# A fused attention, gating-MLP and expert kernel on one core: earlier W_out loads, earlier third-batch input, copies of Q in another order

## The chip, the core and the metric

The kernel runs on one core of a Trainium2 chip. The metric is device time in microseconds, the median of the runs shown. The core has a matrix engine (PE, with its weight loads shown as PEld), three engines for elementwise work (DVE, ACT, POOL) and a queue for transfers on SyncE (SP); ACT issues some transfers too. All of them run at the same time and meet through semaphores.

## What is computed

Three layers in a row, all in float32, with 4 batches of 576 tokens and 512 features:

```python
def reference(q, k, v, ...):
    # stage 1: attention with rotated q and k, 8 heads of 64
    q_rot, k_rot = rotate(q), rotate(k)
    scores = q_rot @ k_rot.T / sqrt(64)
    x = softmax(scores) @ v                      # heads side by side: 4 x 576 x 512
    # stage 2: MLP with a gate over the tokens
    h = gelu(x @ w_in)                           # 512 -> 1024
    u, v = h[..., :512], h[..., 512:]
    v_n = (v - mean(v)) / sqrt(var(v) + 1e-6) * g_ln
    v_s = einsum('ts,bsd->btd', w_sg, v_n) + b_sg
    x = x + (u * v_s) @ w_out
    # stage 3: four experts, each a causal attention with one head of 64; two of four per token
    for e in range(4):
        q, k, v = x @ wq[e], x @ wk[e], x @ wv[e]
        ye = softmax(causal(q @ k.T / 8)) @ v @ wo[e]
        out += weight_of_expert(x @ w_gate, e) * ye
```

## The kernel before

Every product is done in three matmuls: each float32 operand is split into a high part and a low part (`split`: ACT casts the high part, POOL, sometimes DVE, subtracts it for the low part), and `mm3` adds high x high, high x low and low x high. So every tile that PE takes as an operand needs a cast on ACT and a subtraction on POOL or DVE ahead of it. In tile names the letter h is the high part, l the low part: xh and xl are the split input of stage 2, gxh and gxl the split gated product, wuh and wul the split W_out, yh and yl the split input of stage 3, hi and lo those of a projection of Q or K.

PE, ACT, DVE and POOL keep the order in which the program is written while the flag `fixed` is set (class `Engine`), so an instruction that waits holds back all that stand behind it on its engine. Transfers on SP are placed by the scheduler, and SP issues them in that order; a transfer that waits for its source or its buffer holds back those behind it.

Stage 2 is written as units, each a generator that first issues PE's matmuls and then, step by step, the work on the other engines; `unit` advances the two units before it and takes side steps in between. For each batch b there are `values(b, tb)` (five blocks of tokens, matmuls into ps_t and ps_S), `gates_(b, dc)` (four feature chunks, results in the tiles u), `added(b - 1, dc)` (W_out's product of the batch before, plus the input, which is loaded as xr<-xd; the sum is stored to yd) and `mixed(b, dc)` (the product over the tokens, with the weights wsh and wsl and the operands vh and vl, and the gate: DVE scales by gl, adds bs and multiplies by u). Beside the units run side generators:

- `attended(bx, b + 1)`, the next batch's input in twelve steps: load (sa<-xr, sl<-xr, and sr, which is three transfers), norm (a multiplication on POOL, and a store to xd) and part (the split into xh and xl) for each of four chunks. The tiles sa have three buffers. For b = 1 this is the third batch. In the loop over b, the number of steps that a unit takes of it stands in a tuple.
- `leftover`, the last 64 tokens of two batches at once (ea, er, eh, el).
- `lu`, the loading and splitting of W_out by chunks of rows: a transfer on ACT's queue (raw), a conversion by ACT into the scratch bank ps_c, integer steps on DVE in ps_c, then wt, wuh and wul.
- `normalized(b)`, which makes vh and vl from the values.

gl and bs are the gate's scale and offset, loaded by SP and halved by DVE once.

Stage 3 goes through the pairs n = 0 to 7 (two experts of one batch each). `qkproj` makes the projections of Q and K of the next pair; Q's high and low parts are taken to the operands q2 and qz by six transfers on SP (`fill_q`), four of which read hi. The tile hi has one buffer, so the cast of K into hi waits until these four have read it. `parts_of(b)` loads and splits the stage's input (x, then yh and yl) in steps; the table `INPUT_AT` says in which slots of a pair they are taken, its first row for n = 0.

Of the kernel before, what the change touches and what calls it, by code (L numbers as in the profile page):

```python
# [12 lines left out]
ALU = mybir.AluOpType  # L13
AX = mybir.AxisListType

B, H, S, D = 4, 8, 576, 64
# [10 lines left out]
def f(ap):  # L27

    return ap.bitcast(F32)
# [4 lines left out]
QK_AT = (0, 1, 3, 3, 4, 4)  # L34
FINISH_AT = ((7, 8), (4, 5))
VALUES_AT = (1, 4)
INPUT_AT = ((0, 1, 2, 3, 5, 6), (1, 3, 5, 7), (2, 4))


@with_exitstack  # L40
def fused_kernel(ctx, tc, qk, v, w_in, w_out, w_sg, g_ln, b_sg, wqk, wvg, wo, rope, cst, out):
# [17 lines left out]
    PE, ACT, DVE, POOL = Engine(nc.tensor), Engine(nc.scalar), Engine(nc.vector), Engine(nc.gpsimd)  # L59
# [9 lines left out]
    def bank(t):  # L69
        shape = [P, 2, 512] if t.isupper() else [P, 512]  # L70
        return ps[t].tile(shape, F32, tag="b", name="ps_" + t)
# [12 lines left out]
    def halves(t):  # L84
        return [(t[:, c, 0:HS], slice(HS * c, HS * c + HS)) for c in range(2)]
# [12 lines left out]
    def mm3(o, chunks):  # L98


        n = len(chunks)
        for ci, (lh, ll, rh, rl) in enumerate(chunks):
            for pi, (l, r) in enumerate(((lh, rh), (lh, rl), (ll, rh))):
                for (t, sl) in o:
                    PE.matmul(t, l, r[:, sl], start=(ci == 0 and pi == 0),
                              stop=(ci == n - 1 and pi == 2))
            yield


    class Pair:  # L110
# [41 lines left out]
        def fill_q(self, qh, ql):  # L152
            q2, qz = self.q2, self.qz
            a, c = slice(0, 64), slice(64, 128)
            todo = [(q2[a, 0, 0:S], qh[a, :]), (q2[c, 0, 0:S], ql[a, :]), (qz[a, 0], qh[a, :])]
            if self.turned:
                todo += [(q2[c, 1, 64:640], qh[c, :]), (q2[a, 1, 64:640], ql[c, :]), (qz[c, 1], qh[c, :])]
            else:
                todo += [(q2[c, 1, 0:512], qh[c, 0:512]), (q2[a, 1, 0:512], ql[c, 0:512]),
                         (qz[c, 1, 64:S], qh[c, 0:512])]  # L160
                for o, i in ((q2[c, 1, 576:640], qh[c, 512:576]), (q2[a, 1, 576:640], ql[c, 512:576]),
                             (qz[c, 1, 0:64], qh[c, 512:576])):
                    POOL.tensor_copy(o, f(i))
            for (o, i) in todo:
                nc.sync.dma_start(f(o), f(i))
# [93 lines left out]
    def run(gen):  # L259
        for _ in gen:  # L260
            pass
# [83 lines left out]
    with ExitStack() as st:  # L345
# [30 lines left out]
        class Work:  # L376
# [53 lines left out]
            def values(self):  # L430
                self.vst = ld2.tile([P, NKB, 2, P], F32R, tag="vst", name="vst")
                ACT.copy(self.vst[:, :, :, 0:D], self.vt)
                POOL.tensor_tensor(self.vst[:, :, :, D:P], self.vt, f(self.vst[:, :, :, 0:D]), op=ALU.subtract)
# [266 lines left out]
    with ExitStack() as st:  # L700
# [8 lines left out]
        gl = wp.tile([P, 4], F32, name="gl")  # L709
        bs = wp.tile([P, S], F32, name="bs")  # L710
# [137 lines left out]
        def added(b, dc):  # L848

            gh, gll = gs[b]  # L850
            sl = slice(P * dc, P * dc + P)
            t = bank("S")
            xr = wk.tile([P, S], F32, tag="u", name="xr", bufs=5) if dc % 2 else ge.tile([P, S], F32, tag="ga", name="xr", bufs=2)
            nc.sync.dma_start(xr, xd[b][dc])
            run(mm3(halves(t), [(wu[0][:, c, sl], wu[1][:, c, sl], gh[:, c], gll[:, c]) for c in range(4)]))
            yield
            DVE.tensor_tensor(hv(xr), t[:, :, 0:HS], hv(xr), op=ALU.add)
            nc.sync.dma_start(yd[b][dc], xr)
# [4 lines left out]
        def unit(g, *side, then=iter(()), n=0):  # L863


            next(g)
            todo = [s for s, k in side for _ in range(k)]
            a, b = [[t] for t in taken]
            while a or b:
                if a:  # L870
                    x = next(a[0], LATER)
                    if x is LATER:
                        a = []
                if b:
                    if next(b[0], LATER) is LATER:
                        b = []
                if todo:
                    next(todo.pop(0), None)
            for s in todo + n * [then]:
                next(s, None)  # L880
            taken[:] = [g, taken[0]]
# [4 lines left out]
        lu = load_split64(wst, *wu, w_out, 0, nc.scalar.dma_start, POOL, 2, lambda: bank("c"))  # L886
# [3 lines left out]
        at = nsteps  # L890
        for tb in range(2, NKB):
            unit(values(0, tb), (lw, 2), (at, (1, 1, 1)[tb - 2]))
            if tb == 2:
                DVE.tensor_scalar(gl, gl, 0.5, None, op0=ALU.mult)
                DVE.tensor_scalar(bs, bs, 0.5, None, op0=ALU.mult)
        ln = normalized(0)
        unit(gates_(0, 0), (lw, 2), (at, 2))
        unit(gates_(0, 1), (lw, 2), (at, 2))
# [3 lines left out]
        unit(gates_(0, 3), (ln, 2))  # L902
        run(at)
        run(lw)

        for tb in range(2):
            unit(values(1, tb), then=ln, n=1)
# [3 lines left out]
        for b in range(1, B):  # L911
            at = attended(bx, b + 1) if b + 1 < B else iter(())
            for tb in range(0 if b > 1 else 2, NKB - b % 2):
                unit(values(b, tb), (lu, 3), (at, (1, 2, 2, 1, 0)[tb]))
            ln = normalized(b)
            for dc in range(4):
                unit(gates_(b, dc), (lu, 2), (ln, (0, 0, 1, 1)[dc]), then=ln, n=(0, 2, 0, 0)[dc])
            run(lu)
            if b == 2:
                w = wc.tile([P, 12, DM], F32R, tag="w", name="w")  # L920
                wq, wo_ = [w[:, 0:4], w[:, 4:8]], [w[:, 8:10], w[:, 10:12]]
                side = itertools.chain(load_split(wst, *wq, wqk), load_split(wst, *wo_, wo))
            elif b == B - 1:
                wbs.close()
                cr = ExitStack()
                one, ld, cy = [cr.enter_context(tc.tile_pool(name=n, bufs=k, side="right", reuse_waits="tile"))
                               for n, k in (("c_one", 1), ("c_ld", 2), ("c_y", 1))]
                prs3 = [Pair(one, x, ident) for x in range(2)]
                ypools.append(cy)
                xtile[0] = lambda: wst.tile([P, 1024], F32, tag="raw", name="x", bufs=2)[:, 0:640]  # L930
                wg = wtile(one, "wg", 4, 260)
                side = itertools.chain(parts_of(0), load_split(wst, *wg, wvg))
            else:
                side = leftover(bx, b + 1)
            for dc in range(4):
                unit(added(b - 1, dc), (ln, (1, 2, 1, 2)[dc]), (at, (0, 1, 1, 2)[dc]))
            for dc in range(4):
                unit(mixed(b, dc), (at, 1), (side, 5))
            run(at)
            run(side)  # L940
# [8 lines left out]
    with ExitStack() as st:  # L949
# [319 lines left out]
        def slot3(k):  # L1269
# [100 lines left out]
            if (n + 1) // 2 + 1 < B:  # L1370
                if k == 0 or pp and x == 0:
                    ys.append(parts_of((n + 1) // 2 + 1))
                if x in INPUT_AT[min(n, 2 - pp)]:
                    next(ys[-1], None)
# [114 lines left out]
```

## Time and profile before

| | us |
|---|---|
| runs | 713.23, 714.21, 714.75 |
| median | 714.21 |
| profiled execution | 711.89 |
| its span | 710.1 |
| PE busy in the span | 679.1 (96%) |
| DVE, ACT, POOL busy | 493.9, 462.1, 382.3 |

Stage 1 runs to about 285 us of the span, stage 2 from there to about 517 us, and stage 3 to the end. Times below are in microseconds from the start of the span, and all of one profiled execution. A timeline row gives the start, the duration of one merged group of equal instructions, the engine, the line (L55 is the helper that issues everything on the compute engines), the operation with its output and inputs, and the count. Where the engine was idle just ahead of it, the square bracket has the idle time and what ended it. A row of stretches has the busy time of each engine in it, and the clock that was granted to PE as a share of full speed (PEclk).

### The profile page before, as it was taken

Reading aid. Unit: us, or ns where it says so; the run is one execution under the profiler, and the core shown is the slowest. Engines: PE = TensorE matmul, PEld = TensorE weight load, DVE = VectorE, ACT = ScalarE, POOL = GpSimd, SP = SyncE. Lnnn points to the kernel's source line nnn. Section 1 sums busy time; section 2 is a strip of 40 time slices with the busy share of each in tenths; the row PEclk is TensorE's granted clock in tenths of the full one; section 3 lists DMA queues with packets and bytes.
Section 4 is the critical chain, followed back from the end, with each engine's and each line's share of the span. In section 5 each row is a group of like instructions: output and inputs, shape, how many; then the busy total and the mean of one; then the engine's idle time right before and its main releaser. Section 6 shows DMA issues by size and latency. Waiting matters only on the chain.

```text
span 710.1 us, 13966 instructions
## 1 busy us (share of the span) xinstructions
PE 679.1 (96%) x4813; PEld 608.0 (86%) x4813; DVE 493.9 (70%) x1063; ACT 462.1 (65%) x1110; POOL 382.3 (54%) x353
## 2 busy tenths in 40 slices
PE   7799999999999999999999999999998989999996
PEld 6688887878788888798898799899998979999875
DVE  5797879898979888487873574565247666656674
ACT  7687878878788888574472362572146666666673
POOL 1889788888899873661536507306222443342320
PEclk9899999999999999999999999999999999999999
DMA  8568898878887865562365424045455354442521
GB/s 305 158 160 233 252 292 255 231 230 247 245 240 237 230 179 144 167 176 66 107 199 175 137 79 135 29 134 153 114 169 133 88 149 114 116 124 63 137 83 66
DMA packets 69896, 116.31 MB, mean 164 GB/s; under 512 B 21025, under 2 KB 30082, under 8 KB 69826
## 3 DMA queue, kind: packets, MB, share of 16 engines
q1 hardware_dynamic: 67090, 109.75, 53.9%
q10 hardware_dynamic: 2736, 5.68, 2.6%
q8 instruction: 38, 0.62, 0.4%
q14 instruction: 32, 0.26, 0.1%
HBM read 60.05 MB, written 21.08 MB: 114 GB/s over the span
## 4 chain that ended last, share of the span: by engine, by line
PE 40%; DVE 5%; DMA 2%; ACT 1%; POOL 1%; issue 1%; SPq 1%; ACTq 0%; DVEq 0%
PE ps_S L55 25%; PE ps_o L55 5%; PE ps_f L55 4%; PE ps_t L55 4%; PE ps_s L55 3%; DMA xr<-xd 1%; DVE ps_c L55 1%; DMA yd<-xr 1%; DVE e L55 1%; POOL gxl L55 1%; POOL sa L55 0%; DVE h1l L55 0%; ACT e L55 0%; DVE u L55 0%; DVE xt L55 0%
## 5 line engine op out<-in xcount | busy, mean ns | idle before, releaser
L55 DVE TENSOR_REDUCE nmax<-ps_S 128x1 f32<-128x576 f32 x144 | 107.8, 748 | 26.7 <-PE ps_S L55 26.3
L55 PE MATMUL ps_t<-ident,e 128*128 128x128 f32 x776 | 121.9, 275 | 4.3 <-ACT e L55 2.8
L55 ACT ACTIVATE e<-ps_S,nmax 128x576 f32<-128x576 f32 x144 | 107.5, 746 | 28.3 <-DVE nmax L55 27.1
L55 PEld LDWEIGHTS ps_t<-ident,e 128*128 128x128 f32 x776 | 95.3, 141 | 9.8 <-ACT e L55 4.5
L55 POOL TENSOR_TENSOR t<-t,rp 128x576 f32<-128x576 f32 x61 | 93.0, 1546 | 14.4 <-ACT rp L55 9.2
L55 PE MATMUL ps_S<-kh,q 128*128 128x288 f32 x352 | 81.7, 325 | 11.3 <-ACT e L55 4.2
L55 PEld LDWEIGHTS ps_S<-kh,q 128*128 128x128 f32 x352 | 53.5, 191 | 35.2 <-ACT e L55 18.5
L55 PE MATMUL ps_S<-lo,qz 128*128 128x288 f32 x304 | 66.4, 300 | 1.5 <-DVE lo L55 1.5
L55 POOL TENSOR_TENSOR lo<-t,hi 128x576 fp32r<-128x576 f32 x30 | 42.8, 1428 | 29.2 <-DVE hi L55 15.3
L55 PE MATMUL ps_S<-yh,w 128*128 128x288 f32 x256 | 51.5, 304 | 1.3 <-DVE nmax L55 1.3
L55 ACT ACTIVATE e<-e,nmax 128x128 f32<-128x128 f32 (+4 forms) x72 | 42.2, 586 | 14.0 <-DVE nmax L55 13.8
L55 PEld LDWEIGHTS ps_S<-lo,qz 128*128 128x128 f32 x304 | 49.7, 192 | 1.7 <-DVE lo L55 1.7
L55 POOL TENSOR_TENSOR yl<-x,yh 128x640 fp32r<-128x640 f32 x16 | 25.5, 1594 | 42.7 <-ACT yh L55 40.8
L55 POOL TENSOR_TENSOR t<-t 128x576 f32<-128x576 f32 x29 | 42.5, 1464 | 2.3
L55 PE MATMUL ps_o<-g,v 128*64 128x320 f32 x256 | 41.3, 445 | 0.0
L55 PEld LDWEIGHTS ps_S<-yh,w 128*128 128x128 f32 x256 | 38.7, 189 | 1.5 <-DVE nmax L55 1.5
L55 ACT ACTIVATE ga<-ga 128x512 f32<-128x512 f32 (+1 forms) x34 | 22.3, 656 | 24.0 <-DVE ga L55 23.7
L55 PE MATMUL ps_S<-wsh,vh 128*128 128x288 f32 x160 | 34.6, 298 | 1.7 <-DVE u L55 1.4
L55 POOL TENSOR_TENSOR xl<-sa,xh 128x576 fp32r<-128x576 f32 x12 | 18.2, 1522 | 30.7 <-ACT xh L55 30.7
L55 PE MATMUL ps_S<-wsl,vh 128*128 128x288 f32 x160 | 34.1, 294 | 0.0
L55 POOL TENSOR_TENSOR gxl<-u,gxh 128x576 fp32r<-128x576 f32 x16 | 22.8, 1433 | 19.5 <-ACT gxh L55 19.5
L55 DVE CUSTOM_DVE_ANT_0 e<-ps_s,mask 128x128 f32<-128x128 f32 (+3 forms) x64 | 30.9, 482 | 3.2 <-PE ps_s L55 2.9
(302 smaller groups left out, 2020.6 us busy)
## 6 DMA issues: line engine op xcount, KB each, us to landing
t<-in_qk_dram SPq DMA_DIRECT2D x32, 576.0 KB
kh<-hi SPq DMA_DIRECT2D x92, 144.0 KB
q<-hi SPq DMA_DIRECT2D x38, 144.0 KB
qz<-hi SPq DMA_DIRECT2D x38, 144.0 KB
q<-lo SPq DMA_DIRECT2D x38, 144.0 KB
v<-in_v_dram SPq DMA_DIRECT2D x16, 320.0 KB
sa<-xr SPq DMA_DIRECT2D x16, 288.0 KB
xd<-sa SPq DMA_DIRECT2D x16, 288.0 KB
```

Source lines behind the costliest of these rows:

```text
L55: ins = op(*a, **k)
```

## The change

Four edits: the first row of `INPUT_AT`; the order of the six transfers in `fill_q`; the place of the halving of gl and bs, together with one more step of `lu` ahead of it; and the tuples that give the third batch's input its steps.

```diff
@@ -34,7 +34,7 @@
 QK_AT = (0, 1, 3, 3, 4, 4)
 FINISH_AT = ((7, 8), (4, 5))
 VALUES_AT = (1, 4)
-INPUT_AT = ((0, 1, 2, 3, 5, 6), (1, 3, 5, 7), (2, 4))
+INPUT_AT = ((0, 1, 2, 3, 4, 6), (1, 3, 5, 7), (2, 4))
 
 
 @with_exitstack
@@ -152,12 +152,13 @@
         def fill_q(self, qh, ql):
             q2, qz = self.q2, self.qz
             a, c = slice(0, 64), slice(64, 128)
-            todo = [(q2[a, 0, 0:S], qh[a, :]), (q2[c, 0, 0:S], ql[a, :]), (qz[a, 0], qh[a, :])]
+            todo = [(q2[a, 0, 0:S], qh[a, :]), (qz[a, 0], qh[a, :])]
             if self.turned:
-                todo += [(q2[c, 1, 64:640], qh[c, :]), (q2[a, 1, 64:640], ql[c, :]), (qz[c, 1], qh[c, :])]
+                todo += [(q2[c, 1, 64:640], qh[c, :]), (qz[c, 1], qh[c, :]), (q2[a, 1, 64:640], ql[c, :])]
             else:
-                todo += [(q2[c, 1, 0:512], qh[c, 0:512]), (q2[a, 1, 0:512], ql[c, 0:512]),
-                         (qz[c, 1, 64:S], qh[c, 0:512])]
+                todo += [(q2[c, 1, 0:512], qh[c, 0:512]), (qz[c, 1, 64:S], qh[c, 0:512]), (q2[a, 1, 0:512], ql[c, 0:512])]
+            todo.append((q2[c, 0, 0:S], ql[a, :]))
+            if not self.turned:
                 for o, i in ((q2[c, 1, 576:640], qh[c, 512:576]), (q2[a, 1, 576:640], ql[c, 512:576]),
                              (qz[c, 1, 0:64], qh[c, 512:576])):
                     POOL.tensor_copy(o, f(i))
@@ -890,9 +891,6 @@
         at = nsteps
         for tb in range(2, NKB):
             unit(values(0, tb), (lw, 2), (at, (1, 1, 1)[tb - 2]))
-            if tb == 2:
-                DVE.tensor_scalar(gl, gl, 0.5, None, op0=ALU.mult)
-                DVE.tensor_scalar(bs, bs, 0.5, None, op0=ALU.mult)
         ln = normalized(0)
         unit(gates_(0, 0), (lw, 2), (at, 2))
         unit(gates_(0, 1), (lw, 2), (at, 2))
@@ -902,6 +900,9 @@
         unit(gates_(0, 3), (ln, 2))
         run(at)
         run(lw)
+        next(lu)
+        DVE.tensor_scalar(gl, gl, 0.5, None, op0=ALU.mult)
+        DVE.tensor_scalar(bs, bs, 0.5, None, op0=ALU.mult)
 
         for tb in range(2):
             unit(values(1, tb), then=ln, n=1)
@@ -911,7 +912,7 @@
         for b in range(1, B):
             at = attended(bx, b + 1) if b + 1 < B else iter(())
             for tb in range(0 if b > 1 else 2, NKB - b % 2):
-                unit(values(b, tb), (lu, 3), (at, (1, 2, 2, 1, 0)[tb]))
+                unit(values(b, tb), (lu, 3), (at, (1, 2, 2 if b > 1 else 3, 1 if b > 1 else 2, 0)[tb]))
             ln = normalized(b)
             for dc in range(4):
                 unit(gates_(b, dc), (lu, 2), (ln, (0, 0, 1, 1)[dc]), then=ln, n=(0, 2, 0, 0)[dc])
@@ -933,7 +934,7 @@
             else:
                 side = leftover(bx, b + 1)
             for dc in range(4):
-                unit(added(b - 1, dc), (ln, (1, 2, 1, 2)[dc]), (at, (0, 1, 1, 2)[dc]))
+                unit(added(b - 1, dc), (ln, (1, 2, 1, 2)[dc]), (at, ((0, 1, 1, 2) if b > 1 else (1, 2, 2, 2))[dc]))
             for dc in range(4):
                 unit(mixed(b, dc), (at, 1), (side, 5))
             run(at)
```

The order of the instructions moves at more places than the diff names. On ACT, at the end of batch 0 in stage 2, the first two loads of W_out (`raw<-in_w_out_dram`) and the first conversion (`ps_c<-raw`). Before:

```order
L55 ACTIVATE ga<-ga 128x576
L55 ACTIVATE ga<-ps_S 128x576
L55 ACTIVATE ga<-ga 128x576
L55 ACTIVATE vh<-gv,m,y 128x512
L55 ACTIVATE gv<-gv,m,y 128x512
L55 ACTIVATE ga<-ps_t 128x512
L55 ACTIVATE ga<-ga 128x512
L55 CAST vh<-g_4417 64x512
L55 ACTIVATE ga<-ps_S 128x512
L228 DMA raw<-in_w_out_dram 128x1024 x2
L55 ACTIVATE ps_c<-raw 128x512
```

With the change:

```order
L55 ACTIVATE ga<-ga 128x576
L229 DMA raw<-in_w_out_dram 128x1024 x2
L55 ACTIVATE ga<-ps_S 128x576
L55 ACTIVATE ga<-ga 128x576
L55 ACTIVATE vh<-gv,m,y 128x512
L55 ACTIVATE gv<-gv,m,y 128x512
L55 ACTIVATE ga<-ps_t 128x512
L55 ACTIVATE ga<-ga 128x512
L55 CAST vh<-g_4415 64x512
L55 ACTIVATE ga<-ps_S 128x512
L55 ACTIVATE ps_c<-raw 128x512
```

The pair of loads passes eight instructions.

On POOL, in the units of batch 1 in stage 2, the third batch's input (sa, xl), the split W_out (wul) and the split leftover and gated product (el, gxl). Before:

```order
L55 TENSOR_TENSOR sa<-sa,sr 128x576
L55 TENSOR_TENSOR xl<-sa,xh 128x576 x2
L55 TENSOR_TENSOR ea<-ea,er 128x512
L55 TENSOR_TENSOR el<-ea,eh 128x512
L55 TENSOR_TENSOR xl<-sa,xh 128x576
L55 TENSOR_TENSOR gxl<-u,gxh 128x576
L55 TENSOR_TENSOR sa<-sa,sl 128x256
L55 TENSOR_TENSOR gxl<-u,gxh 128x576
L55 TENSOR_TENSOR sa<-sa,sr 128x576
L55 TENSOR_TENSOR gxl<-u,gxh 128x576
L55 TENSOR_TENSOR xl<-sa,xh 128x576
```

With the change:

```order
L55 TENSOR_TENSOR sa<-sa,sr 128x576
L55 TENSOR_TENSOR xl<-sa,xh 128x576 x3
L55 TENSOR_TENSOR sa<-sa,sl 128x256
L55 TENSOR_TENSOR sa<-sa,sr 128x576
L55 TENSOR_TENSOR xl<-sa,xh 128x576
L55 TENSOR_TENSOR ea<-ea,er 128x512
L55 TENSOR_TENSOR el<-ea,eh 128x512
L55 TENSOR_TENSOR gxl<-u,gxh 128x576 x4
```

All four xl of the third batch, and the two steps on its last sa, now stand ahead of ea and of the gxl.

On SP, at the same place, the stores of batch 0's results (yd_0 to yd_3), the loads of its input (xr<-xd) and the load of the third batch's last chunk (sa<-xr_65). Before:

```order
L858 DMA yd_2_89<-xr 128x576
L854 DMA xr<-xd_3_74 128x576
L272 DMA x<-yd_0_87 128x576
L273 DMA x<-yd_0_87 128x64
L272 DMA x<-yd_1_88 128x576
L273 DMA x<-yd_1_88 128x64
L327 DMA ea<-xr_65 128x4x64
L327 DMA ea<-xr_66 128x4x64
L858 DMA yd_3_90<-xr 128x576
L294 DMA sa<-xr_65 128x576
```

With the change:

```order
L859 DMA yd_1_88<-xr 128x576
L859 DMA yd_2_89<-xr 128x576
L295 DMA sa<-xr_65 128x576
L855 DMA xr<-xd_3_74 128x576
L273 DMA x<-yd_1_88 128x576
L328 DMA ea<-xr_65 128x4x64
L328 DMA ea<-xr_66 128x4x64
L274 DMA x<-yd_1_88 128x64
L295 DMA sa<-xr_66 128x576
L296 DMA sl<-xr_66 128x256
L859 DMA yd_3_90<-xr 128x576
```

The load of the last chunk stands behind the store yd_2 instead of yd_3 and ahead of the load xr<-xd_3 that the fourth sum needs. In `fill_q`, the last copy that reads hi goes from the sixth place to the fourth, as the diff shows.

## Rows read from the trace of the kernel before

**Rows 1.** Page, part 1: busy time, share of the span, instructions.

```profile
PE 679.1 (96%) x4813; PEld 608.0 (86%) x4813; DVE 493.9 (70%) x1063; ACT 462.1 (65%) x1110; POOL 382.3 (54%) x353
```

**Rows 2.** Timeline of PE, 325 to 350: start, duration, operation, idle before.

```profile
325.99 0.53 PE L55 MATMUL ps_S<-wsh,vh 128*128 128x288 f32 x2 [0.30 <-DVE vh L55]
...
331.88 0.50 PE L55 MATMUL ps_S<-wsh,vh 128*128 128x288 f32 x2 [1.36 <-DVE u L55]
...
349.14 0.80 PE L55 MATMUL ps_S<-x,wih 128*128 128x288 f32 x4 [0.78 <-DVE gv L55]
```

**Rows 3.** Timeline of DVE, 300 to 346.

```profile
300.14 0.95 DVE L55 TENSOR_SCALAR gl<-gl 128x4 f32<-128x4 f32 x1 [0.53 <-DMA gl<-in_g_ln_dram]
301.01 0.46 DVE L55 TENSOR_SCALAR bs<-bs 128x576 f32<-128x576 f32 x1
...
329.52 0.70 DVE L55 TENSOR_SCALAR ps_c<-ps_c 128x512 f32<-128x512 f32 x1 [1.45 <-ACT ps_c L55]
...
345.07 1.43 DVE L55 TENSOR_SCALAR ps_c<-ps_c 128x512 f32<-128x512 f32 x2 [1.28 <-ACT ps_c L55]
```

**Rows 4.** Timeline of ACT and its transfer queue (ACTq), 324 to 329.

```profile
324.54 0.33 ACTq L228 DMA_DIRECT2D raw<-in_w_out_dram  x1
...
328.84 0.65 ACT L55 ACTIVATE ps_c<-raw 128x512 f32<-128x512 f32 x1 [3.14 <-DMA raw<-in_w_out_dram]
```

**Rows 5.** Timeline of PE, 386 to 395.

```profile
386.57 0.39 PE L55 MATMUL ps_t<-wih,xh 128*128 128x512 f32 x1
386.80 0.39 PE L55 MATMUL ps_t<-wil,xh 128*128 128x512 f32 x1
...
391.91 0.79 PE L55 MATMUL ps_t<-wih,xl 128*128 128x512 f32 x1 [1.29 <-POOL xl L55]
...
394.98 0.39 PE L55 MATMUL ps_S<-wih,xh 128*128 128x512 f32 x1
```

**Rows 6.** Stretch 392 to 394: length, PE, PEld, DVE, ACT, POOL, PEclk, DMA.

```profile
392.00:394.00 2.00, 2.00 (x5) 1.61 (x6) 0.63 (x1) 0.60 (x1) 1.92 (x3) 0.50 0.77 187
```

**Rows 7.** Timeline of SP's queue, 370 to 378.

```profile
370.45 0.33 SPq L858 DMA_DIRECT2D yd<-xr  x1
...
377.82 0.43 SPq L294 DMA_DIRECT2D sa<-xr  x1
```

**Rows 8.** Timeline of DVE, 371 to 425.

```profile
371.05 0.69 DVE L55 TENSOR_TENSOR vh<-g,vh 64x512 fp32r<-64x512 f32 x1
376.66 0.76 DVE L55 TENSOR_TENSOR xr<-ps_S,xr 128x576 f32<-128x576 f32 x1 [4.92 <-DMA x<-yd]
...
424.60 1.45 DVE L55 TENSOR_TENSOR vl<-gv,vh 128x512 fp32r<-128x512 f32 x1
```

**Rows 9.** Timeline of POOL, 390 to 425.

```profile
390.46 1.39 POOL L55 TENSOR_TENSOR xl<-sa,xh 128x576 fp32r<-128x576 f32 x1
...
424.06 1.44 POOL L55 TENSOR_TENSOR xl<-sa,xh 128x576 fp32r<-128x576 f32 x1 [21.48 <-ACT xh L55]
```

**Rows 10.** Timeline of ACT in stage 3, pairs 0 and 2.

```profile
532.44 0.61 ACT L55 ACTIVATE e<-e,nmax 128x384 f32<-128x384 f32 x1 [0.69 <-DVE nmax L55]
...
579.14 0.64 ACT L55 CAST hi<-ps_S 128x576 fp32r<-128x576 f32 x1 [2.80 <-DMA q<-hi]
```

**Rows 11.** Timeline of PE in stage 3, the same pairs.

```profile
539.32 0.53 PE L55 MATMUL ps_S<-yh,w 128*128 128x288 f32 x2 [1.30 <-DVE nmax L55]
...
580.63 0.79 PE L55 MATMUL ps_S<-kh,q 128*128 128x288 f32 x4 [0.98 <-DVE lo L55]
...
582.08 0.66 PE L55 MATMUL ps_t<-ident,e 128*128 128x128 f32 x4 [0.40 <-ACT e L55]
```

**Rows 12.** Timeline of PE at the first mixed unit of batch 1.

```profile
374.84 0.43 PE L55 MATMUL ps_S<-wsh,vh 128*128 128x288 f32 x2
```

**Rows 13.** Timeline of SP's queue, copies of Q for pair 2.

```profile
574.01 0.59 SPq L165 DMA_DIRECT2D q<-hi  x1
...
575.34 0.60 SPq L165 DMA_DIRECT2D qz<-hi  x1
```

## The prediction, made before the changed kernel was run

> **What bounds the kernel now.** I read the page first, then the matrix engine's own timeline with the waits printed behind it, then the timelines of the engines it waited for. The page [rows 1] gives PE 96% of the span. So an edit is worth only what it takes out of PE's waits or out of its slow stretches, and the rest of the working is a search for those within reach of the diff.
>
> In the stretch where the second stage starts, PE stops three times [rows 2]: 0.30 us at 325.99, 1.36 us at 331.88 and 0.78 us at 349.14, each for DVE. DVE itself was idle 1.45 us at 329.52 and 1.28 us at 345.07, both for ACT's conversion of W_out into the scratch bank ps_c [rows 3]. ACT in turn sat 3.14 us until 328.84 for the first W_out load, which it had issued only at 324.54 [rows 4]. DVE and ACT keep their program order, so a conversion step that waits holds back the gate behind it; that is the chain to PE's 1.36 us.
>
> The dearest spot lies at 387 to 395 [rows 5]. PE works on the third batch's values there and needs its fourth input chunk. The last of its waits is 1.29 us at 391.91, for POOL's xl; another, of about one microsecond, stands just before it. What follows is dearer than the wait: in 392 to 394 the granted clock was 0.50, that is the lower of the two levels, 1.2 GHz [rows 6]. I count the loss whole. The ps_t matmul at 386.57 is the first of this batch, the ps_S matmul at 394.98 the nineteenth. The first two follow each other by 0.23 us (386.57 to 386.80), and so do the other undisturbed ones, so the nineteenth was due at 386.57 + 18 x 0.23 = 390.71. It came 4.27 us late.
>
> Why the chunk is late: SP issued its load (sa<-xr) only at 377.82, behind a store of a result that DVE had first to add [rows 7]. That add, at 376.66, had waited 4.92 us for a load [rows 8]. POOL then takes the chunk in among other work, and its low part comes at 390.46 [rows 9].
>
> In the third stage the pair n=2 is held up at 578 to 583. ACT's hi cast of K at 579.14 waited 2.80 us for the copies that read Q's hi, since both use one buffer [rows 10]; PE waited 0.98 us at 580.63 and 0.40 us at 582.08 [rows 11]. Another stop, 1.30 us at 539.32 for DVE's maximum, belongs to the pair n=0 [rows 11].
>
> **Part by part.** *The scaling of gl and bs.* It leaves 300.14 and 301.01, where it costs 0.95 + 0.46 us, and stands behind the third vl, shortly before the wait at 325.99. Nothing waits for its result before the first gate near 330. Moving it gives DVE 1.41 us at one place and takes it at the other; the wait at 325.99 shows that the later place has no spare time on the way to the vh that PE needs. DVE waits for ACT in between, so most of the gift upstream will be lost and part of the debt too. I take 0, with bounds -0.30 (that wait goes) and +1.1 (1.41 less the 0.30 that shifts with it).
>
> *W_out earlier.* The first two loads pass eight ACT instructions, as the order of ACT shows. If six of them ran ahead of the issue at 324.54 (the queue runs a little ahead of the engine), each of the kind that took 0.65 us at 328.84 [rows 4], the issue comes at least 3.9 us sooner, near 320.6. The first load took 328.84 - 324.54 = 4.30 us from issue to use, and would be there by 324.9 or earlier; ACT's turn for it comes at 328.84 - 3.14 = 325.7. ACT's wait goes, and DVE's idle 1.45 us with it. But one more conversion step now stands ahead of the gate: two TENSOR_SCALAR in a row instead of one, the extra one costing 0.70 us [rows 3]. Net 0.75 from this, and a little more because ACT goes on without having waited: I take 0.9 us of the 1.36. Bounds 0.4 and 1.36.
>
> All later W_out steps are one step earlier too, so the step which held DVE at 345.07 lies before the values' work and no longer in it. I take the whole 0.78 us at 349.14; bounds 0 and 0.78. The cover for this is that the load of the third and fourth W_out chunk keeps its distance to its step; if it does not, the wait just stays.
>
> *Third batch's input.* All twelve steps are now done before the first mixed of batch 1; before, four lay in the mixed units and one behind them. What counts is the queue: SP's sa<-xr of the fourth chunk now stands directly behind the store of the third result (370.45 in the old timeline [rows 7]) and ahead of the load for the fourth add. It also needs a buffer that the first chunk's xl leaves, and that xl comes sooner now. So I put the issue between 370.5 and 373 instead of 377.82, and nothing but an addition and a multiplication on POOL, a cast and a subtraction stand between landing and use. Before, from issue to the end of the subtraction (390.46 + 1.4 = 391.9) took 14 us, with ea, el and three gxl in between. Even these 14 us would end between 384.5 and 387, and the first use is not due before 386.57 + 9 x 0.23 = 388.6. I expect it well ahead of that, and take the whole 4.27 us. Bounds: 3.0 (a short stop with the slower clock behind it) and 4.27.
>
> What pays for it: ACT has three xh casts in front of the last vh of batch 1. A cast of this size takes 0.64 us (the hi of [rows 10]), together 1.9 us. DVE made that vh at 371.05, done at 371.74 [rows 8], and PE takes it at 374.84 [rows 12]. The spare 3.1 us hides the casts, so they cost nothing. If that cover goes, each further microsecond is one of PE's. The second thing that is moved is POOL's xl, three of 1.44 us, which now run beside DVE's vl. Where that already happens in batch 2, with the POOL xl at 424.06 [rows 9], the vl at 424.60 took 1.45 us [rows 8] where 0.69 is usual for such an operation. Two or three such stretches cost 0.8 us each, 1.5 to 2.3 in all. Together with the casts that is 3.4 to 4.2 us against a cover of 3.1. Since the two delays partly run at the same time on different engines, and batch 2 has the same pattern and no PE wait there, I take 0, with +1.2 as the bound.
>
> On this the Trainium skill has a rule, in "SBUF — State Buffer", section "Who interferes with whom": a VectorE instruction with two SBUF inputs contends with a GpSimd instruction that reads SBUF, and whoever has the shared ports locks the other out. The vl is of that kind and its 1.45 us agrees. Taken at its word, with three xl fully blocking three DVE operations, the cost would be 3 x 1.44 = 4.3 us in place of my 1.5 to 2.3, and the sum 1.2 to 3.1 us smaller; it is the second rival below.
>
> *Copies of Q in another order.* The four copies that read hi come first. In the stretch of n=2 the last of them was the sixth issue, at 575.34; it takes the place of the fourth, at 574.01 [rows 13], 1.33 us earlier. ACT's cast can then start near 577.8, and both PE waits (0.98 + 0.40 = 1.38) hang on it. I take 1.3; bounds 0.7 (a landing that is set by the amount of data rather than by the issue) and 1.38. The copies that read lo come later by the same, but lo has a buffer that nobody waits for there. In the first stage PE has no wait at these copies, so nothing is gained.
>
> *Split one slot earlier.* ACT's yh moves in front of the exponential at 532.44, which had 0.69 us of idle time ahead of it [rows 10]. From the hi cast's 0.64 us for 576 columns I estimate 0.7 us for its 640. That just fits into the idle time if its input has landed, and leaves the next two exponentials 0.7 us freer. If the input is late, the exponential waits for it, and up to the whole 0.7 us falls on the path. Between -0.7 and +0.7 I take 0; the wait of 1.30 us at 539.32 stays.
>
> **Sum**: 0 - 0.9 - 0.78 - 4.27 + 0 - 1.3 + 0 = -7.3 us. The profiled execution took 711.89 us (span 710.1), 2.3 us under the median of 714.21, as the timed ones scatter by about one. I apply the difference to both: 704.6 for a profiled run, 714.2 - 7.3 = **706.9 us** as the median.
>
> **Rivals.** (1) The fourth chunk stays late. The wait moves to another link, for instance the sa buffer, or a transfer held behind a store that waits at the head of SP's queue. Against it: the room worked out above, even with the old 14 us. Then only 0.9 + 0.78 + 1.3 = 3.0 us go: 711.2 us.
>
> (2) Ports shared by DVE and POOL. The blocked vl and vh of batch 1 arrive after PE at 374.84. At 1.2 us, the gain is 6.1: 708.1. At the 4.3 us of full blocking plus 1.9 of casts, less 3.1 of cover, it is 3.1 us of stall and the gain 4.2: 710.0 (three xl of 1.44 us, each keeping DVE out for its whole length). For it speaks the 1.45 at 424.60; against it, that batch 2 has no stall.
>
> (3) Slower than before. SP is one queue, and the xd store of the second chunk now stands ahead of the first two xr<-xd loads, which feed the adds of batch 0. If POOL is late with that chunk, the adds wait, DVE waits with them in order, and the vl and vh of batch 1 with it. The cover at 374.84 is 3.1 us; an arrival later by 3.1 + 7.3 = 10.4 us, or some 8.5 where the slower clock behind a long stop adds its two microseconds (as at 392 to 394), makes the kernel slower. At 12 us late it would be 714.2 - 7.3 + 8.9 + 2 = 717.8 us. Against it, POOL had idle time in that stretch, and the conversion it used to wait for comes earlier.
>
> (4) Everything goes, also the 0.30 and the 1.30 at 539.32, and the full 1.36 and 1.38: 714.2 - 9.4 = 704.8.
>
> **Chances and range.** The forecast (706.9, itself 705.6 to 708.5) 0.60; rival 2 between 708 and 710 0.14; rival 1 at 711.2 0.12; rival 4 0.06; a new stall that eats the gain up to no change 0.04; rival 3 0.04. The range runs from 704.3 to 711.4. A measurement here tells about 0.2%, 1.4 us, from no change, so faster means under 712.8: 0.92; within it 0.04; slower 0.04.
>
> **What would show it.** PE has no wait on xh or xl between 380 and 390 and the granted clock is 1.00 throughout; SP's sa<-xr of the fourth chunk is issued directly behind a yd store; the stop of 1.36 us is half a microsecond and the one at 349 is gone; ACT waits about 1.5 instead of 2.8 us for the Q copies of n=2. The prediction is wrong if a new wait on vh or u stands at the first mixed of batch 1, or if PE still waits for xl.

## The result, and the profile after

The changed kernel took 705.34 us (median of 5 runs, 704.82 to 707.46) against 713.23 before: a ratio of 0.991, with a 95% interval from 0.9884 to 0.9936. That is 6.4 us less by the ratio (4.6 to 8.3; the two medians lie 7.9 us apart). The forecast was 7.3 us, and 705.34 is inside its range. Timed a second time beside the experiments, it took 704.79 (ratio 0.9909, 0.9881 to 0.9938).

The profiled execution took 704.99 us. Its page (first the span, then busy time, share and count of each engine) shows the same work as [rows 1] in a span that is 6.9 us shorter:

```profile
span 703.2 us, 13972 instructions
...
PE 677.8 (96%) x4813; PEld 608.8 (87%) x4813; DVE 492.2 (70%) x1063; ACT 463.0 (66%) x1110; POOL 383.5 (55%) x353
```

To see where it came from, I laid each trace beside that of the kernel before and took, matmul by matmul in PE's order, the start in the one minus the start in the other. Where this shift changes, time was won or lost. By stretches, in us (stage 1 is where no edit was meant to act; W_out and scaling: 310 to 370 of the old timeline; third batch: 370 to 400; pairs 0 and 2 of stage 3: 525 to 545 and 575 to 590):

| kernel | stage 1 | W_out, scaling | third batch | pair 0 | pair 2 | behind it |
|---|---|---|---|---|---|---|
| forecast | 0 | -1.68 | -4.27 | 0 | -1.3 | 0 |
| the change, trace 1 | -0.96 | -2.03 | -4.35 | +1.69 | -1.46 | +0.14 |
| the change, trace 2 | +0.97 | -2.14 | -4.34 | +1.90 | -1.21 | +0.20 |
| the change, trace 3 | +1.44 | -2.05 | -4.35 | +1.83 | -1.28 | -0.39 |
| the change, trace 4 | -0.02 | -2.04 | -4.34 | +1.91 | -1.20 | -0.01 |

The first column is the first lesson: the same code reaches the end of stage 1 at times that differ by 2.4 us, so one trace's span says little and the stretches say much. The middle columns repeat within 0.3 us between these four traces. Three of them are near the forecast; pair 0 is not. Without stage 1 the columns add up to 5.6 to 6.2 us, against the 7.25 of the forecast.

At the start of stage 2, PE's stops are now these (timeline of PE; in brackets the idle time and its releaser), to be laid beside [rows 2]:

```profile
324.83 0.53 PE L55 MATMUL ps_S<-wsh,vh 128*128 128x288 f32 x2 [0.30 <-DVE vh L55]
...
329.90 0.51 PE L55 MATMUL ps_S<-wsh,vh 128*128 128x288 f32 x2 [0.54 <-DVE u L55]
```

The 0.30 us has stayed, 1.36 has become 0.54, the 0.78 us at 349 is gone. DVE's timeline shows the trade ahead of the gate: no idle time, but two conversions, where [rows 3] has one behind 1.45 us of idle time:

```profile
326.83 1.41 DVE L55 TENSOR_SCALAR ps_c<-ps_c 128x512 f32<-128x512 f32 x2
328.15 0.82 DVE L55 SCALAR_TENSOR_TENSOR ps_S<-ps_S,gl,bs 128x576 f32<-128x576 f32 x1
```

In the third batch's stretch PE has no gap and the full clock, against 0.50 in [rows 6] (stretch: length, busy time of PE, PEld, DVE, ACT and POOL, PEclk, DMA share, GB/s):

```profile
380.00:395.00 15.00, 15.00 (x79) 13.03 (x79) 8.61 (x14) 5.31 (x9) 9.38 (x9) 1.00 0.39 116
```

SP now issues the fourth chunk's load straight behind the stores yd_1 and yd_2, at 366.83 and not at 377.82 as in [rows 7] (SP's queue):

```profile
364.61 2.13 SPq L859 DMA_DIRECT2D yd<-xr  x2
366.83 0.38 SPq L295 DMA_DIRECT2D sa<-xr  x1
```

### The profile page after: what moved, and what is told of

It reads as the page before. It is cut to its first block, busy times and chain, and to the rows that moved or that the text cites. A ratio compares the mean times of both kernels' runs of the same rounds, so it can differ in the third digit from the quotient of the medians.

```text
span 703.2 us, 13972 instructions
## 1 busy us (share of the span) xinstructions
PE 677.8 (96%) x4813; PEld 608.8 (87%) x4813; DVE 492.2 (70%) x1063; ACT 463.0 (66%) x1110; POOL 383.5 (55%) x353
## 4 chain that ended last, share of the span: by engine, by line
PE 75%; DVE 13%; ACT 6%; DMA 3%; issue 2%; POOL 1%; SPq 0%; ACTq 0%; POOLq 0%; DVEq 0%
PE ps_S L55 43%; PE ps_o L55 14%; PE ps_t L55 11%; PE ps_f L55 4%; DVE nmax L55 2%; PE ps_s L55 2%; DVE wt L55 2%; DMA kh<-hi 2%; ACT e L55 1%; DVE e L55 1%; PE ps_l L55 1%; ACT qz L55 1%; DVE g L55 1%; DVE g01l L55 1%; POOL t L55 1%
```

## The experiments

Each of the first four undoes one part of the change. The same shifts, for the runs told of below:

| kernel | stage 1 | W_out, scaling | third batch | pair 0 | pair 2 | timed, ratio to before (95%) |
|---|---|---|---|---|---|---|
| split undone, trace 1 | -1.39 | -2.10 | -4.34 | +0.67 | -1.09 | 703.32, 0.9877 (0.9855 to 0.9899) |
| split undone, trace 2 | +2.03 | -1.71 | -4.34 | -0.67 | -1.32 | |
| split undone, trace 3 | -1.95 | -1.67 | -4.34 | -0.68 | -1.52 | |
| copies undone | +0.64 | -1.52 | -4.34 | +0.26 | -0.44 | 706.62, 0.9915 (0.9889 to 0.9942) |
| third batch undone | -0.59 | -2.09 | -2.98 | +1.85 | -0.87 | 706.93, 0.9923 (0.9900 to 0.9945) |
| W_out, scaling undone | -0.32 | -0.53 | -4.35 | +0.29 | -1.29 | 707.32, 0.9931 (0.9907 to 0.9956) |
| scaling alone undone | +1.48 | -1.68 | -4.34 | +1.80 | -1.51 | 706.74, 0.9929 (0.9908 to 0.9951) |
| third batch alone | -0.03 | -0.55 | -4.34 | 0.00 | -0.25 | 707.30, 0.9950 (0.9923 to 0.9976) |
| last split later | -1.28 | -2.12 | -4.34 | -1.88 | -1.23 | 701.40, 0.9858 (0.9825 to 0.9891) |

**The split undone.**

```diff
-INPUT_AT = ((0, 1, 2, 3, 4, 6), (1, 3, 5, 7), (2, 4))
+INPUT_AT = ((0, 1, 2, 3, 5, 6), (1, 3, 5, 7), (2, 4))
```

> The change, but with the first row of INPUT_AT as before (the cast of the third chunk of the next batch's input stays behind the exponential). Theory: the moved cast has to wait for its input's transfer (ACT idle 0.97 us in the trace of the change), makes the stop at pair 0 0.30 us longer, and with that longer stop PE's clock falls, which costs 1.39 us more. So the PE's shift at 545 us returns by 1.7 us: profiled span 701.5, 1.7 us less than the change's 703.2, and no stretch at 0.5 of the clock near 532. Rival A: the clock falls there by chance, whatever the cast does; then only 0.3 us is gained (702.9) and the slow stretch shows in some runs of both. Rival B: the cast takes nothing; no difference.

703.32 us, and the profiled span came out at the expected 701.5, but by luck: the clock fell here too, and 0.43 us of the 1.7 come from stage 1. In the change, ACT's moved cast waits for its input, and the exponential behind it starts without the spare time of [rows 10] (timeline of ACT):

```profile
524.86 0.73 ACT L55 CAST yh<-x 128x640 fp32r<-128x640 f32 x1 [0.97 <-DMA x<-yd]
525.50 0.61 ACT L55 ACTIVATE e<-e,nmax 128x384 f32<-128x384 f32 x1
```

PE's three stops at pair 0 are 0.87, 0.88 and 1.30 us, and then the clock falls to the lower level, 0.50 (timeline of PE, then stretches, both of the change):

```profile
528.63 0.66 PE L55 MATMUL ps_t<-ident,e 128*128 128x128 f32 x4 [0.87 <-ACT e L55]
...
530.34 0.66 PE L55 MATMUL ps_t<-ident,e 128*128 128x128 f32 x4 [0.88 <-ACT e L55]
532.29 0.85 PE L55 MATMUL ps_S<-yh,w 128*128 128x288 f32 x2 [1.30 <-DVE nmax L55]
```

```profile
532.00:534.00 2.00, 1.71 (x7) 1.71 (x8) 1.63 (x8) 1.73 (x6) 0.23 (x1) 0.50 0.64 168
534.00:536.00 2.00, 2.00 (x14) 2.00 (x12) 0.60 (x3) 0.12 (x2) 0.00 (x0) 0.65 0.03 8
```

With the split undone the stops are shorter, and still the clock fell there in this trace; its matmul at 530.83 takes 0.85 us as well:

```profile
527.43 0.66 PE L55 MATMUL ps_t<-ident,e 128*128 128x128 f32 x4 [0.17 <-ACT e L55]
...
529.13 0.66 PE L55 MATMUL ps_t<-ident,e 128*128 128x128 f32 x4 [0.88 <-ACT e L55]
530.83 0.85 PE L55 MATMUL ps_S<-yh,w 128*128 128x288 f32 x2 [1.04 <-DVE nmax L55]
```

So the theory that the longer first stop is what brings the clock down fell. That the moved cast costs time without any help of the clock was still to be shown.

**Four more traces, two of the change and two with the split undone.**

> The change itself, a third trace. Both traces so far had PE's clock at half for some 3 us behind the stops of pair 0 (532 to 535, 535 to 538). Theory: chance, so that one of the looks of this call keeps the full clock with the same three waits (0.9, 0.9, 1.3), and the next matmuls come 1.4 to 1.6 us sooner. Rival: it belongs to the longer stop which the moved split makes, and every trace of the change shows it.

> The change itself, a fourth trace. Theory: the clock at pair 0 falls by chance, in some traces of the same kernel and not in others. Rival: it falls in every trace of the change.

> The change with the first row of INPUT_AT as before, a second trace. Its first one had the shorter first wait (0.17) and half the clock all the same. Theory: chance, some of its traces keep the clock. Rival: the clock falls here in all traces of this version too, and what keeps it in the kernel before is something else.

> The change with the first row of INPUT_AT as before, a third trace. Theory: the clock at pair 0 falls by chance, in some traces and not in others. Rival: it falls in every trace of this version.

Both of the change lost the clock at pair 0 (+1.83 and +1.91), both with the split undone kept it (-0.67 and -0.68). One of the latter (trace 2), PE's timeline and the stretch:

```profile
531.24 0.66 PE L55 MATMUL ps_t<-ident,e 128*128 128x128 f32 x4 [0.17 <-ACT e L55]
...
534.63 0.53 PE L55 MATMUL ps_S<-yh,w 128*128 128x288 f32 x2 [1.03 <-DVE nmax L55]
```

```profile
534.00:536.00 2.00, 1.37 (x10) 1.37 (x11) 1.62 (x8) 1.39 (x5) 0.23 (x1) 1.00 0.74 225
```

Over all traces: with the moved split the clock fell in six of eight (the two that kept it are "copies undone" and "W_out, scaling undone"), with the split at its old place in one of five (the kernel before and "third batch alone" kept it). So the fall is not bound to the edit: it came and stayed away on either side, with the same waits. Whether the edit makes it more frequent, 13 traces can't tell, since counts at least as uneven come by chance in about one case of twelve. What is shown is its price, 1.3 to 1.6 us: 1.69 to 1.91 against 0.29 where the waits are the same, and +0.67 against -0.67. The moved cast alone, with the full clock on both sides, costs 0.96 us (+0.29 against -0.67).

**The copies undone** (`fill_q` as before, in both stages).

```diff
-            todo = [(q2[a, 0, 0:S], qh[a, :]), (qz[a, 0], qh[a, :])]
+            todo = [(q2[a, 0, 0:S], qh[a, :]), (q2[c, 0, 0:S], ql[a, :]), (qz[a, 0], qh[a, :])]
...
```

> The change, but with the six copies of Q in the order of before, in stages 1 and 3. Theory: the stop at pair 2 of stage 3 comes back, PE 1.4 us later there (ACT idle 2.8 instead of 1.3 us ahead of the cast of K); the 0.96 us by which the first stage ended sooner in the trace of the change is start-up scatter and stays: total about 1.4 us slower than the change. Rival: the copies also make stage 1 quicker; then stage 1 ends 0.96 us later as well, 2.4 us in all. Rival 2: the moved cast at pair 0 waits for less or more since its load stands behind the same six copies: no difference at pair 2, some tenths at pair 0.

At pair 2 both of PE's stops stand, 0.55 and 0.40 us:

```profile
575.22 0.79 PE L55 MATMUL ps_S<-kh,q 128*128 128x288 f32 x4 [0.55 <-DVE lo L55]
...
576.68 0.66 PE L55 MATMUL ps_t<-ident,e 128*128 128x128 f32 x4 [0.40 <-ACT e L55]
```

With the change ACT's cast of K there waits less than half as long as the 2.80 us of [rows 10]:

```profile
572.03 0.64 ACT L55 CAST hi<-ps_S 128x576 fp32r<-128x576 f32 x1 [1.30 <-DMA qz<-hi]
```

The first of the two stops is gone in all eleven traces with the new order. The second fell below 0.2 us in three of them only and stayed at 0.31 to 0.41 in eight, such as the change's trace 2:

```profile
577.26 0.66 PE L55 MATMUL ps_t<-ident,e 128*128 128x128 f32 x4 [0.41 <-ACT e L55]
```

The new order is worth about 1.0 us there, not the expected 1.4: -0.87 to -1.52 in the eleven traces with it, 0, -0.25 and -0.44 in the three without. The timed 706.62 us is not clear of the change's 704.79 (the intervals overlap).

The rival on stage 1 finds no support, though its end scatters too much (-1.95 to +2.03 us) to exclude some tenths. In the traces of the old order SP already issues the four copies of hi ahead of those of lo in eight of stage 1's 15 blocks, so the edit alters seven, the first at 77 us. From 60 us to the end of stage 1 the shift changes by -1.03 to +2.97 us with the new order (mean +0.2) and by -0.46 to +0.42 with the old.

**The third batch undone** (both tuples as before).

```diff
-                unit(values(b, tb), (lu, 3), (at, (1, 2, 2 if b > 1 else 3, 1 if b > 1 else 2, 0)[tb]))
+                unit(values(b, tb), (lu, 3), (at, (1, 2, 2, 1, 0)[tb]))
...
-                unit(added(b - 1, dc), (ln, (1, 2, 1, 2)[dc]), (at, ((0, 1, 1, 2) if b > 1 else (1, 2, 2, 2))[dc]))
+                unit(added(b - 1, dc), (ln, (1, 2, 1, 2)[dc]), (at, (0, 1, 1, 2)[dc]))
```

> The change, but with the steps of the third batch's input as before. Theory: the stop for the fourth chunk near 390 us of the old timeline comes back with its slow clock, 4.3 us more than the change. Rival: the earlier W_out steps already free POOL and SP, the stop is shorter and clear of the clock: 1 to 3 us more.

The rival held. Only 1.37 us of the 4.35 come back (-2.98 is left). PE has one stop and keeps the full clock behind it (timeline, then a stretch), and POOL does its work in the old order, from ea to the last xl:

```profile
387.64 0.50 PE L55 MATMUL ps_t<-wih,xl 128*128 128x512 f32 x1 [1.06 <-POOL xl L55]
```

```profile
388.00:390.00 2.00, 2.00 (x10) 1.67 (x9) 0.69 (x1) 1.07 (x2) 1.92 (x3) 1.00 0.83 195
```

```profile
375.28 1.28 POOL L55 TENSOR_TENSOR ea<-ea,er 128x512 f32<-128x512 f32 x1 [4.31 <-DMA ea<-xr]
...
386.16 1.42 POOL L55 TENSOR_TENSOR xl<-sa,xh 128x576 fp32r<-128x576 f32 x1
```

From ea's start to the end of xl are 12.3 us, as in the kernel before (379.56 to 391.85): the same work in the same order. It starts 4.28 us earlier, while PE's own shift there is only 2.68 us. POOL's lead begins with a W_out step: its wul ahead of that work starts at 355.62 us and not at 359.40, 1.1 us more than PE's shift. The order in which things follow says that POOL, and with it the stores and loads of SP, has got 1.6 us ahead of PE through the earlier W_out steps; two stops and a slow stretch have become one short stop. No run has the W_out edit without the others, but the copies and the split act in stages 1 and 3.

**The third batch alone** (the kernel before with these two tuples of the change).

> The kernel before with the third batch's steps alone of the change. Theory: the stop for the fourth chunk and the slow clock behind it go whole, whatever W_out does: 4.3 us less than before at that place (no wait on xh or xl near 389), nothing elsewhere: about 708.5. Rival: without the earlier W_out steps POOL is late with the second and third sa, SP with the loads behind their stores, and a part of the stop stays.

Ratio 0.9950: 3.6 us, with the whole 4.34 of it in its place, and no gap and the full clock:

```profile
380.00:395.00 15.00, 15.00 (x87) 13.45 (x86) 6.93 (x11) 5.87 (x10) 12.88 (x11) 1.00 0.36 111
```

So either edit takes most of this stop, 4.34 us for the third batch's steps alone or 2.98 without them, and together they take 4.35: they overlap. The theory held and the rival fell.

**W_out and scaling undone.**

```diff
-        next(lu)
-        DVE.tensor_scalar(gl, gl, 0.5, None, op0=ALU.mult)
-        DVE.tensor_scalar(bs, bs, 0.5, None, op0=ALU.mult)
```

(the two scalings stand again behind `unit(values(0, 2), ...)`)

> The change, but with the W_out load and the scaling of gl and bs as before. Theory: the stops of 1.36 and 0.78 us come back in place of 0.54 and 0: 0.8 + 1.0 = 1.8 to 2.0 us more than the change. Rival: with the third batch's input earlier, the later W_out steps hold POOL and SP up as well, and the stop for the fourth chunk returns in part: 3 us or more.

PE's stops are 0.84 and 0.74 us where the change has 0.54 and none:

```profile
331.04 0.51 PE L55 MATMUL ps_S<-wsh,vh 128*128 128x288 f32 x2 [0.84 <-DVE u L55]
...
348.28 0.81 PE L55 MATMUL ps_S<-x,wih 128*128 128x288 f32 x4 [0.74 <-DVE gv L55]
```

The edit is worth 1.5 us against the four traces of the change (-0.53 against -2.03 to -2.14), not the expected 1.8 to 2.0, and 1.0 to 1.6 over all traces with it (-1.52 to -2.14) and the two without it beside the kernel before (-0.53 and -0.55). The rival fell: the third batch's stop stays away (-4.35). The half microsecond by which these two differ from the kernel before is that kernel's own: the stop of 1.36 us in [rows 2] was a long one. It is 0.84 here and 0.80 in "third batch alone", with W_out's load at the old place in both, because that load took 3.8 us to its use here (324.22 to 328.00) and 4.30 in [rows 4].

**The scaling alone undone** (its two lines at the old place, `next(lu)` kept).

> The change, but with the scaling of gl and bs at its old place; the first step of W_out stays early. Theory: the place of the scaling is worth nothing within 0.3 us, the waits at 325 and 330 of the trace stay at 0.30 and 0.54. Rival: the old place, where DVE waited 0.53 us for gl, pushes the whole start of stage 2 back by up to 0.6 us, or the new one does, and taking it away frees the 0.30 us.

-1.68 against -2.03 to -2.14, 0.35 to 0.45 us. It shows as one more stop ahead of the 0.30 us that stays:

```profile
326.80 0.53 PE L55 MATMUL ps_S<-wsh,vl 128*128 128x288 f32 x2 [0.28 <-DVE vl L55]
...
327.64 0.53 PE L55 MATMUL ps_S<-wsh,vh 128*128 128x288 f32 x2 [0.30 <-DVE vh L55]
```

But "copies undone" (0.43 us) and the traces 2 and 3 of "split undone" (0.23 and 0.29) have such a stop too, with the scaling at its new place, and their stretch is -1.52 to -1.71. So no worth of the scaling is shown beyond the scatter; it lies between 0 and 0.45 us. The waits of 0.30 and 0.54 stayed, as the theory had it.

**The last split later.**

```diff
-INPUT_AT = ((0, 1, 2, 3, 4, 6), (1, 3, 5, 7), (2, 4))
+INPUT_AT = ((0, 1, 2, 3, 5, 7), (1, 3, 5, 7), (2, 4))
```

> The change, but with the first row of INPUT_AT as (0, 1, 2, 3, 5, 7): the split of the third chunk stands where it stood before, that of the fourth one slot later than in either kernel. Theory: the wait of 1.04 to 1.30 us for DVE's maximum at pair 0 comes from the comparison of the experts (eq, cmp), which is held while POOL's second yl reads SBUF; with that yl gone behind it, the comparison takes 0.24 + 0.24 us, the wait falls to at most 0.1 us, and with only one stop of 0.9 us left the clock does not fall: 1.3 us (up to 2.7 with the clock) less than the version with the split undone, about 701.5 to 702 as a median. Rival: the wait is for the matmuls of the block itself, DVE's maximum waits for something else, and nothing changes: 703.3.

This kernel has the lowest median, 701.40 us, ratio 0.9858 (0.9825 to 0.9891); all its four runs (700.52 to 702.07) lie below all six of the change timed with them (702.93 to 707.29). The theory held: the third stop is gone and the median is within 0.1 us of the forecast. The stop of 1.30 us in [rows 11] is gone in its trace, one of 0.62, for the comparison, is left, and the clock stays at 1.00 (timeline of PE):

```profile
527.52 0.66 PE L55 MATMUL ps_t<-ident,e 128*128 128x128 f32 x4 [0.17 <-ACT e L55]
...
528.98 0.65 PE L55 MATMUL ps_t<-ident,e 128*128 128x128 f32 x4 [0.62 <-DVE cmp L55]
529.70 0.53 PE L55 MATMUL ps_S<-yh,w 128*128 128x288 f32 x2
```

What went is DVE's comparison of the experts, eq and cmp, on 128x80. With the split undone, cmp starts while POOL's two yl run and ends when they end, near 530 (timelines of DVE and POOL of that kernel):

```profile
528.37 0.23 DVE L55 SCALAR_TENSOR_TENSOR eq<-cmp,lower 128x80 f32<-128x80 f32 x1
528.64 1.46 DVE L55 SCALAR_TENSOR_TENSOR cmp<-cmp,eq 128x80 f32<-128x80 f32 x1
```

```profile
526.73 3.26 POOL L55 TENSOR_TENSOR yl<-x,yh 128x640 fp32r<-128x640 f32 x2 [0.61 <-ACT yh L55]
```

With the last split later, POOL's yl lies behind the comparison, and both take a quarter of a microsecond:

```profile
528.46 0.23 DVE L55 SCALAR_TENSOR_TENSOR eq<-cmp,lower 128x80 f32<-128x80 f32 x1
528.73 0.24 DVE L55 SCALAR_TENSOR_TENSOR cmp<-cmp,eq 128x80 f32<-128x80 f32 x1
```

```profile
526.83 1.56 POOL L55 TENSOR_TENSOR yl<-x,yh 128x640 fp32r<-128x640 f32 x1 [0.62 <-ACT yh L55]
...
530.74 1.57 POOL L55 TENSOR_TENSOR yl<-x,yh 128x640 fp32r<-128x640 f32 x1
```

The rule of the Trainium skill that the prediction weighed elsewhere ("SBUF — State Buffer", section "Who interferes with whom") bears on this place: a VectorE instruction with two inputs in SBUF and a GpSimd instruction that reads SBUF keep each other out. Here the trace agrees: 1.46 us in place of 0.24. Pair 0 stands at -1.88 us, 1.2 us better than the -0.67 of the split undone, with the full clock in both.

**The change once more**, timed beside these.

> The change itself, once more, beside the others of this call. In its first trace PE's clock was at half for about 3 us behind the stops of pair 0 (532 to 535), which cost 1.39 us; the version with the W_out edit undone had the same three waits there (0.86, 0.88, 1.30) and kept the full clock, and the one with the split undone had a shorter first wait and lost the clock. Theory: the fall of the clock there is chance, so this trace may show it or not, and the median lies at 705.3 as before. Rival: it belongs to the change and shows again, in each run, 1.4 us.

704.79 us, and the clock at pair 0 at half again. So it fell in all four traces of the change, as the rival had it; that it belongs to the change is not shown by that, since two other kernels with the moved split kept it.

## Why the prediction was right, and where it was not

*The total.* Forecast 7.3 us, measured 6.4 (4.6 to 8.3). It is right as a total; one of its terms, the split, lay outside its bounds, and one, the third batch, was right for only part of its reason. That the total lies so near is in part luck: the split took 1.7 to 1.9 us, the start of stage 2 gave 0.4 more than its terms, and the rest is within the scatter of the runs.

*The scaling.* Taken as 0, bounds -0.30 to +1.1. Measured 0 to 0.45 in its favour, not told from 0. The wait of 0.30 us stayed in every trace. DVE's gl took 0.16 us at the new place and not the 0.95 of [rows 3], so the debt was smaller than reckoned.

*W_out earlier.* 0.9 of the 1.36 us, and it was 0.82; the 0.78 us went whole. Mechanism and size were right, down to the second conversion that stands ahead of the gate. Part of the 1.36 was a late load in the one trace that the sum rested on: the edit's own worth, with the scaling, is 1.0 to 1.6 us, not 1.68.

*Third batch.* 4.27 forecast, 4.34 to 4.35 measured; load at the place in SP's queue, no wait and full clock as listed. The issue came even sooner than forecast, at 369.8 us of the old timeline (366.83 plus the shift of 3.0) and not between 370.5 and 373. The unspoken step was that this gain belongs to this edit alone. The change without it takes 2.98 of it, which the sum, adding edits one by one, didn't ask. The sum came out right since the two together can't take more than the stop.

*The covers at the first mixed unit.* Rival 2 fell. POOL's three xl did lengthen DVE's work beside them (timelines of POOL and DVE of the change):

```profile
364.11 4.68 POOL L55 TENSOR_TENSOR xl<-sa,xh 128x576 fp32r<-128x576 f32 x3 [6.13 <-ACT xh L55]
```

```profile
366.31 1.19 DVE L55 TENSOR_TENSOR vl<-gv,vh 128x512 fp32r<-128x512 f32 x1
368.07 1.27 DVE L55 TENSOR_TENSOR vh<-g,vh 64x512 fp32r<-64x512 f32 x1 [0.57 <-ACT vh L55]
```

That is 0.5 and 0.6 us over the 0.69 of [rows 8], 1.1 us in place of the forecast 1.5 to 2.3 and the 4.3 of a full block. Of the operations on vl and vh only these two met an xl, and each came while one was running, so neither paid for a whole one. POOL paid too: its three xl took 4.68 us, where three of 1.44 make 4.3. The vh is done at 369.34, PE takes it at 371.84 (374.84 in [rows 12], less 3.0): 2.5 us of the 3.1 us of cover are left. Rival 1 and rival 3, on SP's queue, fell with the issue at 366.83.

*Copies of Q.* 1.3 forecast, 1.20 to 1.46 in the traces of the change. By the traces with the old order, 0.25 to 0.44 of that come by themselves in some runs, so the edit is worth about 1.0. Of the mechanism one half held: ACT's cast came sooner and the 0.98 us went, but the 0.40, which the forecast hung on the same cast, mostly stayed. The remark that PE has no wait in the first stage at the copies of Q is right by name but narrow: in the kernel before PE waits 3.5 us there in all for the copies of K (kh<-hi), which pass through the same queue. The new order also seems to have a worth at pair 0 that the forecast didn't have: with the split at its old place, pair 0 stands at -0.67 with the new copies and at 0.00 with the old ones. These traces differ in the W_out edit too, which acts far ahead of this place, so this is argued and not isolated.

*The split.* This is the step that failed. It was taken as 0 with bounds of 0.7 either way, and the change loses 1.69 to 1.91 us there in each of its four traces. Two things were missed. First, the term took the spare 0.69 us ahead of the exponential as cover for the cast and left open whether the input would have landed. It had not: ACT waited 0.97 us for it. The first stop grew from 0.17 to 0.87 us, 0.70 more, and the third from 1.03 to 1.30, where DVE's comparison meets POOL's yl at another point (eq takes 1.51 us in the change, cmp 1.46 with the split undone). So the -0.67 that stands there with the split undone turns into +0.29, 0.96 us in all. Second, the term had no price for the clock behind the stops, though the same prediction had counted just that at 392 to 394. It adds 1.4 to 1.6 us in most traces. Undoing the edit gave 703.32 us in place of 705.34 and 704.79; the intervals overlap, so it is the stretches and not the timed runs that show the loss.

The earlier load that would have made the moved cast free was not tried: the kernel has two buffers of x, which are full until the first split is done. Whether a third would fit and help, no run shows.

## What to carry to other kernels

Lay two traces beside each other instruction by instruction and read the shift by stretch: here the totals of one kernel scattered over four to seven microseconds from run to run, and the stretches repeated within a few tenths. Two edits that free the same wait don't add, so price each also with the other one already made. A cast that is moved into idle time is free only if its input is there, and a tiny DVE instruction with two inputs in SBUF can cost nearly a whole POOL instruction when they meet: moving one POOL split by a slot brought 1.2 us more than undoing the edit alone.

## What the runs showed of the hardware

PE's clock fell at the last of the three stops of pair 0, or within 1 us behind it, in seven of thirteen traces (the kernel before, the four of the change, the three with the split undone, and five others; "last split later" no longer has the three stops). With 0.86, 0.88 and 1.29 us it fell in the change's trace 3; with 0.86, 0.88 and 1.30 it held at 1.00 in "W_out, scaling undone" (third stop, then the stretch behind it):

```profile
534.41 0.54 PE L55 MATMUL ps_S<-yh,w 128*128 128x288 f32 x2 [1.30 <-DVE nmax L55]
```

```profile
534.00:536.00 2.00, 1.59 (x12) 1.59 (x13) 1.62 (x8) 1.61 (x5) 0.22 (x1) 1.00 0.65 164
```

So the waits alone don't decide it. The Trainium skill, "TensorE: Matmul & The Clock Gate", in its part 1 on the clock gate, says that the moment at which the clock rises varies from run to run. It says so of the rise behind a start, and what varied here is whether the clock fell behind the same stops. What tips it here stays open.

The end of stage 1 varied over 4.0 us (-1.95 to +2.03) between traces whose edits hardly touch it, by 2.4 us between four of the same kernel. Much of it lies in PE's waits for the copies of K: they add up to 0.6 us in "last split later" (-1.28) and to 4.7 us in "split undone, trace 2" (+2.03). That makes the span of a single trace a poor measure of an edit of a few microseconds.

A DVE operation on 128x80 with two inputs took 0.23 to 0.24 us alone, and 1.46 to 1.59 us where POOL's yl ran beside it.
